# Chunk-selected attention feeding a top-1 expert layer: the first two head pairs in a new order, weights sent later, and expert tiles of two 64-row parts

## The chip, the core and the metric

The kernel runs on one core of a Trainium2 chip. The core has five engines that run side by side, each with its own queue of instructions: TensorE (PE, matmuls; its weight loads are listed as PEld), VectorE (DVE), ScalarE (ACT), GpSimd (POOL) and SyncE (SP, which only issues transfers). The metric is the device time of one execution in microseconds (us).

## The reference

For 4 batches, 8 heads, 768 positions and head size 64, attention is computed on chunks of 32 keys. Each query takes, of the chunks up to its own, the six with the highest upper bound, and attends to them alone. The rows of all heads (3072 tokens of 512) then go through one of eight experts each.

```python
k_min = np.min(k_chunks, axis=3)
k_max = np.max(k_chunks, axis=3)
ub = np.sum(np.maximum(q[:, :, :, None, :] * k_min[:, :, None, :, :], q[:, :, :, None, :] * k_max[:, :, None, :, :]), axis=-1)
ub = np.where(causal, ub, -1000000000.0)
top_chunks = np.argsort(ub, axis=-1)[..., -top_k:]
scores = scale * np.matmul(q, k.transpose(0, 1, 3, 2))
mask = sel & (pos[:, None] >= pos[None, :])
scores = np.where(mask, scores, -1000000000.0)
...
return np.matmul(attn, v).astype(np.float32)
...
expert_idx = np.argmax(logits, axis=1)
for e in range(E):
    mask = expert_idx == e
    xe = x[mask]
    h = np.maximum(xe @ w1[e], 0.0)
    ye = h @ w2[e]
    out[mask] = gate_w[mask, None] * ye
```

For the inputs of this case the eight experts get 85, 507, 932, 530, 163, 358, 285 and 212 tokens; after three of the four batches 45, 427, 850, 342, 99, 118, 274 and 149.

## The kernel before

**Stage one: 16 head pairs.** A pair is two heads of one batch. For each pair, `k_t` and `q_t` (L237, L266) transpose keys and queries on PE into the one bank `ps_t`; `k_red` (L243) takes each chunk's minimum and maximum on DVE; `k_out` (L261) copies the keys to KTE in four pieces on ACT; `q_v` and `q_va` (L279, L283) copy the queries to qT on DVE or ACT, `q_r` (L287) makes their positive part, `q_c` (L295) their bfloat16 copy on POOL. `kse` (L250) makes the two sides of the bound, `ub` (L382) multiplies them on PE, and `bound`, `maxes`, `choose` (L391 to L402) pick six chunks on DVE. The choice is transposed on PE and put (`put`, `put_to`) into rows 64 to 87 of QSB; the mask rows (`mask_rows`, L121) in the same rows of KTE make the score of a chunk that was not chosen strongly negative. `scores(i, u)` (L426) and `av(i, u)` (L457) do the attention in seven units of 384 queries by 128 keys; `v_t`, `v_c`, `vw`, `vw_c` add the gate's columns to V, and `norm` (L474) writes the rows of tokens.

Scores, sums over V and bounds use 64 columns of weights at a time (CW, L60), in two halves of PE's columns.

**Order.** PE and POOL run in the written order throughout, DVE and ACT too in the opening (L781 to L862). Pair 0 is prepared by `first` (L329) and `select_first` (L354), with idle matmuls (`idle`, L131) in PE's gaps; the keys of pair 1 are transposed after pair 0's choice, and the opening ends with the keys of pair 3 (`keys(3)`, L860). In the loop (L867) pair i is attended to, the bounds of pair i+1 computed, the queries of pair i+2 and the keys of pair i+3 transposed.

**Transfers.** `load` (L212) sends keys, queries and values by SP's queue, about two pairs ahead. `load_w` (L197) sends one of 32 pieces of the expert weights (512 KB as they land) by POOL's queue; `wq` (L751) says in which of a pair's four slots: three in the opening (EARLY), then spread over the pairs, none in the second pair of a later batch. `scatter` (L572) writes finished token rows, grouped by expert, to DRAM by the same queue, in slots of the next batch. POOL's third `q_c` of a pair waits for scatters that were issued in the pair before.

**Stage two: experts.** `table` (L596) counts on DVE how many tiles of 128 rows each expert has: full tiles of the first three batches first (11, NA), the rest (20, NB) after the last batch. Of these 31, 28 (JM) always run; the last three stand behind a branch. For a tile `gather` fetches the rows (POOL), `x_in` transposes them (SP), `up` (L706) and `down` (L724) are sixteen matmuls of 512 columns on all 128 columns of PE, with ACT's relu and a DMA transpose between; the weights' offset is read from `woff` at run time. The tiles overlap: `up(j)` is followed by `down(j - 2)` (L978 to L996).

## Time and profile before

| | us |
|---|---|
| median of 3 runs | 352.33 (351.08 to 354.74) |
| the profiled execution | 352.18 |
| its span, first to last instruction | 350.4 |
| PE busy | 316.2 |
| ACT busy | 205.0 |
| POOL busy | 182.5 |
| DVE busy | 175.0 |

The page also lists 224 matmuls of L731, eight for each of 28 tiles. A span's busy time is a mean over stages with different limits, so each stretch is read by itself. A chain of waits follows the last instruction back to what released it at each step: what stands in it set the time there. "Issue" in it is time in which an engine waited for nothing that the profile shows. The DMA share is the mean busy share of 16 DMA engines; overlapping packets can bring it over 1. Names such as ubp (bounds), kp, qp, vp (transposed keys, queries, values), ps (scores), po (sums over V), vwp (gate columns), ph and py (the halves of an expert tile) are those of the tiles written.

### The profile page before, as it was taken

How to read it: one execution, taken by the hardware profiler on the slowest of the kernel's cores; microseconds unless marked ns; L12 is line 12 of the kernel's file. 1: busy time of each engine (PE TensorE's matmuls, PEld its weight loads, DVE VectorE, ACT ScalarE, POOL GpSimd, SP SyncE). 2: the span in 40 equal slices, each digit the busy share in tenths (PEclk: the TensorE clock that was granted, in tenths of full speed). 3: DMA queues.
4: the chain of work that ended last, by engine and by line, in shares of the span. 5: the costliest groups of instructions: out<-in, count | busy, mean ns of one | idle time of the engine just before them, and what ended most of it. 6: DMA issues, size and time to landing. Idle time of an engine off the chain costs nothing.

```text
span 350.4 us, 12914 instructions
## 1 busy us (share of the span) xinstructions
PE 316.2 (90%) x5206; PEld 231.3 (66%) x5206; DVE 175.0 (50%) x671; ACT 205.0 (59%) x306; POOL 182.5 (52%) x332
## 2 busy tenths in 40 slices
PE   7776999989999969899979997977898999999992
PEld 3556788978988959789868896964343444444340
DVE  8557566756886647677666798555700000000000
ACT  2575777757767847767757765352444444455441
POOL 7631434634356736356655555836477455556232
PEclk9899899999999999999999999999999999999999
DMA  7995898978935999854899584326999999999982
GB/s 205 244 227 111 169 217 159 229 170 164 225 87 125 214 195 204 164 144 125 168 225 183 85 168 116 51 64 143 189 229 210 247 187 230 185 213 157 208 158 72
DMA packets 85979, 60.17 MB, mean 172 GB/s; under 512 B 73115, under 2 KB 73117, under 8 KB 85920
## 3 DMA queue, kind: packets, MB, share of 16 engines
q0 software_dynamic: 11392, 29.42, 41.4%
q1 hardware_dynamic: 74528, 29.91, 38.8%
q8 instruction: 43, 0.70, 0.8%
q14 instruction: 16, 0.13, 0.1%
HBM read 56.14 MB, written 10.51 MB: 190 GB/s over the span
## 4 chain that ended last, share of the span: by engine, by line
PE 68%; DVE 9%; issue 8%; DMA 6%; ACT 3%; POOL 3%; POOLq 1%; DVEq 0%; ACTq 0%; SPq 0%
PE po L469 23%; PE ph L714 9%; PE ps L440 9%; PE py L731 8%; PE ubp L387 5%; PE vp L306 4%; PE qp L271 3%; PE kp L241 3%; DMA xs_dram<-xrow,sli 3%; PE vwp L320 2%; ACT KTE L262 2%; POOL out_dram L738 2%; DMA hT<-h__4868 1%; DVE mm L246 1%; DMA spare<-xs_dram,grow 1%
## 5 line engine op out<-in xcount | busy, mean ns | idle before, releaser
L445 ACT ACTIVATE P<-ps 128x768 f32<-128x768 f32 x144 | 89.7, 666 | 57.5 <-PE ps L440 56.9
L469 PE MATMUL po<-V,P 128*64 128x73 f32 x2688 | 107.8, 229 | 7.6 <-issue 3.4
L469 PEld LDWEIGHTS po<-V,P 128*64 128x64 f32 x2688 | 97.8, 137 | 20.5 <-issue 10.3
L454 POOL TENSOR_SCALAR_AFFINE_SELECT P<-P 128x256 f32<-128x256 f32 x90 | 36.0, 415 | 81.6 <-ACT P L445 81.1
L731 PE MATMUL py<-w_all,hT 128*128 x224 | 52.7, 379 | 3.8 <-DMA hT<-h__5871 2.1
L440 PE MATMUL ps<-QSB,KTE 128*64 128x384 bf16 (+2 forms) x576 | 55.3, 292 | 0.7 <-ACT P L445 0.7
L731 PEld LDWEIGHTS <-hT 128*128 128x128 bf16 x224 | 21.9, 98 | 30.7 <-DMA hT<-h__5871 2.5
L262 ACT ACTIVATE KTE<-kp 64x384 bf16<-64x384 f32 x64 | 38.5, 602 | 4.2 <-PE kp L241 2.6
L297 POOL CAST QSB<-qT 64x384 bf16<-64x384 f32 x62 | 29.6, 502 | 15.2 <-DMA xs_dram<-xrow,sli 7.1
L714 PE MATMUL ph<-w_all,KTE 128*128 x120 | 28.3, 379 | 3.7 <-DVE lg L509 1.5
L246 DVE TENSOR_REDUCE mm<-kp 128x48 f32<-128x768 f32 x32 | 29.1, 946 | 0.9 <-PE kp L241 0.9
L440 PEld LDWEIGHTS <-KTE 128*64 128x64 bf16 x576 | 27.0, 110 | 1.8 <-issue 1.6
L575 POOL DMA_INDIRECT xs_dram<-xrow,sli x21 | 21.5, 1024 | 8.6 <-issue 5.2
L738 POOL DMA_INDIRECT out_dram<-V,ti x14 | 13.8, 988 | 22.0 <-ACT V L737 13.4
L714 PE MATMUL ph<-w_all,QSB 128*128 x104 | 24.6, 379 | 0.0
L314 DVE COPY vT<-vp 128x768 f32<-128x768 f32 x14 | 13.4, 957 | 22.2 <-PE vp L306 22.2
L387 PE MATMUL ubp<-ks,qT 128*64 128x48 f32 x320 | 20.4, 223 | 4.2 <-DVE ks L255 2.9
L714 PEld LDWEIGHTS <-KTE 128*128 128x128 bf16 x120 | 11.6, 97 | 18.3 <-issue 3.0
L387 PEld LDWEIGHTS ubp<-ks,qT 128*64 128x64 f32 x320 | 18.7, 139 | 5.0 <-POOL QSB L297 3.3
L387 PE MATMUL ubp<-kd,qA 128*64 128x48 f32 x320 | 20.5, 224 | 1.4 <-DVE kd L258 1.4
L205 POOL DMA_DIRECT2D w_all<-in_moe_w_dram x32 | 21.1, 661 | 0.2
L387 PEld LDWEIGHTS ubp<-kd,qA 128*64 128x64 f32 x320 | 18.7, 140 | 1.6 <-ACT P L445 1.1
(196 smaller groups left out, 426.2 us busy)
## 6 DMA issues: line engine op xcount, KB each, us to landing
w_all<-in_moe_w_dram POOLq DMA_DIRECT2D x32, 512.0 KB, 6.7
V<-in_v_dram SPq DMA_DIRECT2D x32, 192.0 KB, 5.3
k<-in_k_dram SPq DMA_DIRECT2D x8, 384.0 KB, 3.9
q<-in_q_dram SPq DMA_DIRECT2D x8, 384.0 KB, 4.7
w_all<-in_k_dram SPq DMA_DIRECT2D x8, 384.0 KB, 7.1
w_all<-in_q_dram SPq DMA_DIRECT2D x8, 384.0 KB, 4.3
xs_dram<-xrow,sli POOLq DMA_INDIRECT x21, 7.0
out_dram<-V,ti POOLq DMA_INDIRECT x14
```

What stands on the lines that cost most here:

```text
L205: d = nc.gpsimd.dma_start(out=dst, in_=src.rearrange("(c p) f -> p c f" if n < 2 else "(p c) f -> p c f", p=128))
L246: nc.vector.tensor_reduce(s["mm"][:, n].rearrange("p a c -> p (a c)"), s["kp"].rearrange("p j (c w) -> p c j w", w=CH // KG), AX.XY, (ALU. ...
L262: nc.scalar.activation(kte[0:64, hd, :].rearrange("p (r j z) -> p z r j", z=2, j=KG // 2)[:, z], s["kp"][64 * z:64 * z + 64, :, ts(hd, KR ...
L297: nc.gpsimd.tensor_copy(out=o_, in_=i_)
L387: nc.tensor.matmul(pu[64 * hd:64 * hd + 64, t].rearrange("p z n -> p (z n)"), lhsT=s[nm][:, ds(hd * 384 + t * 64, 64)], rhs=w_[:, hd], sta ...
L440: nc.tensor.matmul(pv[c:c + CW, hd, :], lhsT=kte[:, hd, ds(kb * 128 + c, CW)], rhs=qsb[:, hd, ds(qb * 384 + 384 - w, w)], start=True, stop ...
L445: nc.scalar.activation(P[:, :, ds(c0, w)], pv, AF.Exp)
L454: nc.gpsimd.affine_select(out=pd, in_=pd, pattern=[[0, 2], [1, 2], [2, 64]], compare_op=ALU.is_ge, fill=0.0, base=0, channel_multiplier=-1)
L469: nc.tensor.matmul(po[c:c + CW, t].rearrange("p a d -> p (a d)")[:, ds(hd * VW, VW)], lhsT=P[:, hd, ds(col + c, CW)], rhs=vt[:, kb, ds((1 ...
L575: d = nc.gpsimd.indirect_dma_start(out=xs_dram[:], out_offset=bass.IndirectOffsetOnAxis(ap=sli[:, u:u + 1], axis=0), in_=bst[b][f"xrow{u % ...
L714: nc.tensor.matmul(ph[:, fh, :], lhsT=xT[:, c, :], rhs=w_all[:, ds(wo + (c * F + fh * 512), 512)], start=(c == 0), stop=(c == NDC - 1), sk ...
L731: nc.tensor.matmul(py[:], lhsT=hT[:, c, :], rhs=w_all[:, ds(wo + (W1W + c * DM), DM)], start=(c == 0), stop=(c == NFC - 1))
```

## The change

- **Opening.** The keys of pair 1 are transposed into a score bank (`ps_s`, 2 banks) while pair 0's bounds are prepared, and leave it in pieces until the second score unit of pair 0. Pair 0's gate columns come ahead of its first score. All of pair 0's qT is made by ACT, all of its `q_c` by POOL. `first` and `select_first` are gone; `turn` and `put_half` are called from the order itself.
- **Fourth keys.** The keys of pair 3 are transposed and copied in pair 1 of the loop.
- **Constants.** cbias is made by one iota and one DVE instruction instead of one iota and ten. The mask rows of the second and third KTE are copied from the first by SP's queue; the zero fills of those buffers come after pair 0's `q_c`.
- **Weights.** No piece is sent in the opening's constants. `wq` now has two in pair 0, three in each of pairs 1 to 4, then one, two, two, three, one, three, two, and (with the last three) two, one, one.
- **Expert tiles.** After the 11 full tiles the rest is counted in parts of 64 rows (`part_table`). Seven tiles hold two parts of one expert. Eight mixed tiles hold one leftover part in rows 0 to 63, and in rows 64 to 127 one part of expert 0 to 7. 26 tiles always run, two stand behind the branch. In a mixed tile `up` and `down` issue each matmul twice, on 64 columns of weights each, the halves with different experts' w_all.

```diff
-    NB = NTOK // 128 + E - 1 - NA
+    NF = 9
+    NB = NF + E
     JT = NA + NB
-    JM = JT - 3
+    JM = JT - 2
     WE = 2 * DM * F // 128
     W1W = WE // 2
     WL = (E - 1) * WE
     CW = 64
     VW = D + 1 + E
-    EARLY = 3
...
-    def mask_rows(i):
+    def mask_rows():
         for hd in range(2):
-            nc.vector.tensor_scalar(KTE[i][64:64 + NCH, hd, :], colc[64:64 + NCH, :],
+            nc.vector.tensor_scalar(KTE[0][64:64 + NCH, hd, :], colc[64:64 + NCH, :],
                                     pm64[64:64 + NCH, 0:1], MASKV, ALU.is_equal, ALU.mult)
+
+    def more_mask_rows():
+        for i in (1, 2):
+            nc.sync.dma_start(out=KTE[i][64:64 + NCH], in_=KTE[0][64:64 + NCH])
...
+        iota(cbias[:], [[-4, NT - 1], [1, NCH]], base=-4)
...
-        for t in range(1, NT):
-            thr = const.tile([128, 1], FP32, name=f"thr{t}")
-            nc.vector.tensor_scalar(thr[:], chunk_p[:], float(4 * t), None, ALU.add)
-            nc.vector.tensor_scalar(cbias[:, t - 1, :], iota_c[:], thr[:, 0:1], NEG,
-                                    ALU.is_gt, ALU.mult)
-        mask_rows(0)
-        zero_half(KTE[1])
-        zero_half(KTE[2])
-        zero_half(QSB[1])
+        nc.vector.tensor_scalar(cbias[:], cbias[:], chunk_p[:, 0:1], NEG, ALU.is_gt, ALU.mult)
+        mask_rows()
...
-    def table(first):
...
+    def part_table():
...
+        nc.vector.tensor_scalar(ni[:], cnt[:], 63.0, None, ALU.add)
+        nc.vector.tensor_scalar(ni[:], ni[:], 6, None, ALU.logical_shift_right)
...
+        nc.vector.tensor_scalar(more[:], u0[:, 0:1], float(2 * (JM - NA - E)), None, ALU.subtract)
...
+    def col(j):
+        if j < NA + NF - 2:
+            return j
+        return j + 2 if j < JM else j - E
+
+    def parts(j, wo):
+        if NA + NF - 2 <= j < JM:
+            return ((wo, 0, 64), ((j - (NA + NF - 2)) * WE, 64, 128))
+        return ((wo, 0, 128),)
...
-                nc.tensor.matmul(ph[:, fh, :], lhsT=xT[:, c, :],
-                                 rhs=w_all[:, ds(wo + (c * F + fh * 512), 512)],
-                                 start=(c == 0), stop=(c == NDC - 1), skip_group_check=True)
+                for o_, lo, hi in parts(j, wo):
+                    nc.tensor.matmul(ph[lo:hi, fh, :], lhsT=xT[:, c, lo:hi],
+                                     rhs=w_all[:, ds(o_ + (c * F + fh * 512), 512)],
+                                     start=(c == 0), stop=(c == NDC - 1), skip_group_check=True)
...
-            nc.tensor.matmul(py[:], lhsT=hT[:, c, :], rhs=w_all[:, ds(wo + (W1W + c * DM), DM)],
-                             start=(c == 0), stop=(c == NFC - 1))
+            for o_, lo, hi in parts(j, wo):
+                nc.tensor.matmul(py[lo:hi, :], lhsT=hT[:, c, lo:hi], rhs=w_all[:, ds(o_ + (W1W + c * DM), DM)],
+                                 start=(c == 0), stop=(c == NFC - 1), skip_group_check=True)
...
-    slots = [4 * i + g for i in range(NP - 2) for g in range(4) if i < HP or i % HP != 1]
-    wq = EARLY * [-1] + [slots[n * len(slots) // (NW - 3 - EARLY)] for n in range(NW - 3 - EARLY)] + [4 * NP - 7, 4 * NP - 13, 4 * NP - 11]
+    pieces = {0: (2, 3), 5: (0,), 6: (0, 3), 7: (0, 3), 9: (0,), 11: (0, 3), 12: (0,)}
+    wq = [4 * i + g for i in range(NP - 3) for g in pieces.get(i, (0, 2, 3))] + [4 * NP - 7, 4 * NP - 13, 4 * NP - 11]
...
         load(0, "k")
         load(0, "q")
+        load(1, "k")
         load(0, "v")
         with tc.manual_schedule(engines={DVE, ACT}):
             idle = consts_first()
+            load(1, "q")
             p0, p, pj = prep[0], prep[1], prep[2]
+            p0["k_t"]()
+            load(2, "k")
+            p0["q_t"](ps_s.tile([128, 2, 512], FP32, tag="s", name="pq"))
             load(1, "v")
             load(2, "q")
             load(2, "v")
+            idle(3)
+            p0["k_red"](0)
+            p0["k_red"](1)
+            p0["q_va"]()
+            p0["q_r"]()
+            for n in range(4):
+                p0["q_c"](n // 2, n % 2)
+            zero_half(KTE[1])
+            zero_half(QSB[1])
+            zero_half(KTE[2])
+            more_mask_rows()
+            for n in range(4):
+                p0["k_out"](n // 2, n % 2)
+            p["k_t"](ps_s.tile([128, 2, 512], FP32, tag="s", name="pk"))
+            load(3, "k")
+            idle(6)
+            p0["kse"]()
+            p["k_red"](0)
+            p0["ub"]()
+            idle(2)
+            p0["bound"]()
+            p0["maxes"](1, 3)
+            p0["choose"](1, 3)
+            p0["v_t"]()
+            p["k_out"](0, 0)
+            p["k_out"](0, 1)
+            p0["v_c"](act=True)
+            p0["turn"](0)
+            p0["maxes"](3, 6)
+            p0["choose"](3, 6)
+            p0["put_half"](0)
+            idle(2)
+            p["k_out"](1, 0)
+            p0["vw"](ps_o, "o")
+            p0["vw_c"]()
+            scores(0, 0)
+            p["q_t"]()
+            load(3, "q")
+            p["k_red"](1)
+            p0["turn"](1)
+            p0["put_half"](1)
+            p["k_out"](1, 1)
+            scores(0, 1)
+            p["q_v"]()
+            p["q_r"]()
+            p["kse"]()
+            for n in range(4):
+                p["q_c"](n // 2, n % 2)
             consts_pool()
             consts_last()
+            weights(0)
+            av(0, 0)
             scores(0, 2)
+            pj["k_t"]()
+            load(4, "k")
+            pj["k_out"](0, 0)
+            pj["k_out"](0, 1)
+            av(0, 1)
+            pj["k_red"](0)
             scores(0, 3)
             norm(0, 0)
+            p["ub"]()
+            pj["k_out"](1, 0)
+            pj["k_out"](1, 1)
             scores(0, 4)
             p["bound"]()
             p["maxes"](1, 6)
             p["choose"](1, 6)
+            pj["k_red"](1)
+            weights(1)
             av(0, 2)
             scores(0, 5)
             av(0, 3)
+            weights(2)
             p["mask"]()
             p["put"]()
             scores(0, 6)
+            pj["kse"]()
+            p["v_t"]()
+            p["v_c"](act=True)
             av(0, 4)
             pj["q_t"]()
             load(4, "q")
+            pj["q_va"]()
             pj["q_r"]()
+            weights(3)
             av(0, 5)
...
+            if i == 1:
+                pj["k_t"]()
+                load(5, "k")
...
+            if i == 1:
+                pj["k_out"](0, 0)
+                pj["k_out"](0, 1)
```

**ACT in the opening.** KTE are the keys' copies of pairs 0, 1 and 2 (by number), pq the queries of pair 0, P the exponentials. Before, from the first copy on:

```order
L285 ACTIVATE qT<-pq 128x384
L289 ACTIVATE qA<-qT 128x768
L262 ACTIVATE KTE_105<-kp 64x384 x4
L301 ACTIVATE QSB_108<-qT 64x2x3x64 x2
L312 ACTIVATE vT<-vp 128x768
L445 ACTIVATE P<-ps 128x768
L445 ACTIVATE P<-ps 128x2x256
L445 ACTIVATE P<-ps 128x2x128
L262 ACTIVATE KTE_106<-kp 64x384 x4
```

Now, with pk for the keys of pair 1 in the score bank:

```order
L289 ACTIVATE qT<-pq 128x768
L293 ACTIVATE qA<-qT 128x768
L266 ACTIVATE KTE_107<-kp 64x384 x4
L266 ACTIVATE KTE_108<-pk 64x384 x2
L312 ACTIVATE vT<-vp 128x768
L266 ACTIVATE KTE_108<-pk 64x384
L408 ACTIVATE P<-ps 128x768
L266 ACTIVATE KTE_108<-pk 64x384
L408 ACTIVATE P<-ps 128x2x256
L408 ACTIVATE P<-ps 128x2x128
```

Three of pair 1's four copies moved ahead of the first exponential, the fourth ahead of the second.

**DVE at the first bounds.** mm are the key extremes, lo, ks and kd the sides of the bound, ubm the masked bounds. Before:

```order
L123 TENSOR_SCALAR KTE_105<-colc,pm_93 24x768 x2
L246 TENSOR_REDUCE mm<-kp 128x48 x2
L281 COPY qT<-pq 128x384
L253 COPY lo<-mm 64x96
L255 TENSOR_TENSOR ks<-mm,lo 64x2x24 x2
L256 TENSOR_TENSOR lo<-mm,lo 64x48
L258 TENSOR_TENSOR kd<-lo,ks 64x2x24 x2
L394 TENSOR_TENSOR ubm<-ubp,cbias 128x240
```

Now:

```order
L170 TENSOR_SCALAR cbias<-cbias,chunk_p 128x120
L125 TENSOR_SCALAR KTE_107<-colc,pm_92 24x768 x2
L250 TENSOR_REDUCE mm<-kp 128x48 x2
L257 COPY lo<-mm 64x96
L259 TENSOR_TENSOR ks<-mm,lo 64x2x24 x2
L260 TENSOR_TENSOR lo<-mm,lo 64x48
L262 TENSOR_TENSOR kd<-lo,ks 64x2x24 x2
L250 TENSOR_REDUCE mm<-pk 128x48
L357 TENSOR_TENSOR ubm<-ubp,cbias 128x240
```

The copy of qT left DVE, and one of the two reductions of pair 1's keys stands ahead of the masked bounds.

**PE in a tile behind the first 18.** These are the first matmuls of `up`, the ISA rows add up an address. Before:

```order
L707 TENSOR_LOAD woff
L714 ISA
L714 MATMUL ph<-w_all,KTE_107 128x512
L714 LDWEIGHTS KTE_107
L714 ISA
```

Now, in the first mixed tile:

```order
L762 TENSOR_LOAD woff
L770 ISA
L770 MATMUL ph<-w_all,KTE_109 64x512
L770 LDWEIGHTS KTE_109
L770 MATMUL ph<-w_all,KTE_109 64x512
L770 LDWEIGHTS KTE_109
L770 ISA
```

Each matmul became two, on 64 columns of weights; the second has a fixed address.

## Rows read from the trace of the kernel before

**Rows 1.** The page, busy us, share of the span and instructions of each engine.

```profile
PE 316.2 (90%) x5206; PEld 231.3 (66%) x5206; DVE 175.0 (50%) x671; ACT 205.0 (59%) x306; POOL 182.5 (52%) x332
```

**Rows 2.** Table by stretch: length, busy us of each engine, granted clock, DMA share, GB/s.

```profile
9.00:18.00 9.00, 7.04 (x68) 4.74 (x69) 5.28 (x23) 4.87 (x8) 5.61 (x22) 0.81 1.15 242
...
18.00:27.00 9.00, 6.47 (x115) 4.88 (x111) 4.66 (x12) 7.50 (x13) 3.37 (x8) 1.00 0.93 211
...
27.00:39.75 12.75, 10.64 (x201) 9.47 (x201) 8.52 (x31) 7.57 (x13) 2.87 (x6) 0.87 0.59 129
...
53.40:66.10 12.70, 12.70 (x299) 11.22 (x297) 8.62 (x31) 9.59 (x16) 6.72 (x15) 1.00 0.88 174
...
250.80:348.00 97.20, 90.92 (x417) 40.50 (x414) 5.34 (x33) 44.84 (x53) 52.36 (x52) 1.00 0.94 193
```

**Rows 3.** Chain of waits, opening: start us, us, what.

```profile
6.98 1.82 DVE mm L246 x2
...
8.80 0.46 DVE qT L281
...
11.23 1.66 PE ubp L387 x36
...
17.79 0.45 PE ps L440 x4
...
20.17 0.60 ACT KTE L262
```

**Rows 4.** Timeline: start us, us, engine, line, operation, in brackets idle before.

```profile
5.07 0.83 PE L241 MATMUL kp<-ident_f,k 96*128 96x96 f32 x8
...
12.93 0.41 DVE L394 TENSOR_TENSOR ubm<-ubp,cbias 128x240 f32<-128x240 f32 x1 [1.85 <-PE ubp L387]
...
15.49 0.58 DVE L350 COPY QSB<-pm 24x256 bf16<-24x256 bf16 x2 [0.46 <-PE pm L360]
...
39.75 0.82 PE L320 MATMUL vwp<-wgb,vT 128*64 128x16 f32 x24
...
53.40 0.83 PE L320 MATMUL vwp<-wgb,vT 128*64 128x16 f32 x24
```

**Rows 5.** Chain of waits, pairs 2 to 4.

```profile
61.18 0.91 PE po L469 x24
...
62.70 0.81 PE kp L241 x8
...
65.19 0.33 PE ps L440 x4
...
70.26 1.32 issue
...
83.80 1.15 PE ubp L387 x40
```

**Rows 6.** Chain of waits, experts: two halves of tiles.

```profile
250.84 1.73 PE ph L714 x8
...
252.57 1.73 PE py L731 x8
```

**Rows 7.** Timeline of DVE and POOL around the second table.

```profile
246.64 0.15 DVE L600 TENSOR_TENSOR cnt<-base_e,ebase 128x8 f32<-128x8 f32 x1
...
252.86 0.18 DVE L655 SCALAR_TENSOR_TENSOR grow<-inv,loc 128x20 int32<-128x20 f32 x1
...
267.49 1.04 POOL L681 DMA_INDIRECT KTE<-xs_dram,grow  x1 [0.30 <-issue]
```

**Rows 8.** DMA queues in pair 2 (53.40 to 66.10): packets, MB, share.

```profile
q0 software_dynamic: 478, 1.00, 50.1%
...
q1 hardware_dynamic: 1824, 1.18, 37.0%
```

**Rows 9.** Chain of waits and PE's timeline in pair 7.

```profile
118.07 8.87 DMA xs_dram<-xrow,sli
...
128.94 0.88 PE L306 MATMUL vp<-ident_f,V 128*128 128x128 f32 x6 [2.72 <-ACT qT L285]
```

More of the change, by code (lines that the diff above doesn't have):

```diff
@@ L101 @@
     base_e = const.tile([128, E], FP32)
-    jio = const.tile([128, NB], FP32)
+    jio = const.tile([128, NA], FP32)
+    pos = const.tile([128, NB], FP32)
+    p64 = const.tile([128, 1], FP32)
+    upper = const.tile([128, 4, E], FP32)
     tri8 = const.tile([128, E, E], FP32)
@@ L178, in consts_pool @@
         iota(ebase[:], [[NTOK, E]])
-        iota(jio[:], [[1, NB]])
+        iota(jio[:], [[1, NA]])
+        iota(upper[:, 0], [[1, E]])
+        for z in range(2):
+            iota(pos[64 * z:64 * z + 64, 0:NF], [[2, NF]], base=z)
+            iota(p64[64 * z:64 * z + 64, :], [[0, 1]], mul=1)
         for b in range(B):
@@ L799 @@
-            idle(2)
-            def filler():
-                idle(2)
-                p["k_t"]()
-                idle(2)
-            p0["select_first"](filler, idle, lambda: scores(0, 0), lambda: p["k_red"](0))
-            p["k_red"](1)
-            scores(0, 1)
-            load(3, "k")
-            for n in range(4):
-                p["k_out"](n // 2, n % 2)
-            p0["vw"]()
-            p0["vw_c"]()
-            scores(0, 2)
-            av(0, 0)
-            p["q_t"]()
-            load(3, "q")
@@ L974 @@
             tok(5)
-            for _ in table(False):
-                pass
+            part_table()
             def tiles(lo, hi):
@@ L997 @@
         dve.__exit__(None, None, None)
-    rest = nc.values_load(more[0:1, 0:1], min_val=NA - JM, max_val=JT - JM,
-                          skip_runtime_bounds_check_because="the table counts at most one part tile per expert")
+    rest = nc.values_load(more[0:1, 0:1], min_val=-2 * (NF - 2), max_val=4,
+                          skip_runtime_bounds_check_because="every expert leaves one part to a tile of its own")
     with tc.If(rest > 0):
```

292 lines of the change are left out of this document (149 added, 143 removed).

## The prediction

> **What bounds the kernel now.** I read the page's busy times first: TensorE (PE) works for 316.2 of 350.4 us, the next engine (ScalarE, ACT) for 205.0 [rows 1]. Then the table by stretch, which shows where it does not work: 7.0, 6.5 and 10.6 us of the stretches 9 to 18, 18 to 27 and 27 to 39.75 us, with a mean granted clock of 0.81, 1.00 and 0.87 there (part of the first and the last at 1.2 GHz, with gaps in PE's work before) [rows 2]. From 39.75 us, where the first pair of the steady loop adds its gate columns, PE is full: one pair takes 12.7 us where nothing disturbs it. From 250.8 us on the experts run at PE's pace, 90.9 busy us of 97.2 [rows 2]. So three things can move the time: the first 40 us (latency), the disturbed pairs, and the number of expert tiles. The chain of waits tells what orders the first stage [rows 3], the timeline gives its marks [rows 4], the chain of an undisturbed pair gives the price of PE's pieces [rows 5].
>
> **Opening, up to the first score.** Before, the score of pair 0 starts at 17.79 [rows 3]. Step by step in the new order:
> - The key extremes (L246) can start when the eight transposes end, 5.07 + 0.83 = 5.90 [rows 4], where they started at 6.98 [rows 3]: ten small VectorE (DVE) instructions for cbias become one, and the mask rows end earlier. Minus 1.08.
> - The copy of half of qT leaves DVE: minus 0.46 [rows 3]. ACT now makes all of qT and is done long before.
> - The bounds took 1.66 us for 36 pieces at the low clock [rows 3]; at the high one 40 take 1.15 [rows 5]. Second keys and six idle matmuls stand in PE's wait, so I take the high clock: minus 0.5.
> - So the bounds end near 10.9 in place of 12.9. From the start of the adds (12.93) to the end of the first put (15.49 + 0.58 = 16.07) lie 3.1 us [rows 4]; the same DVE work needs some 2.7, since PE's V transposes now hide under the maxima. First put done at 13.6, score at 13.7. Gone between put and score (16.07 to 17.79) are the second keys' transposes and four idle matmuls.
>
> That is 4.1 us. **From the first score to 39.75** lay 22.0 us. PE's work in the new order, at the high clock: four sets of transposes (queries and values of pair 1, keys and queries of pair 2) at 0.81, bounds 1.15, mask 0.3, eight score units at 0.33, seven sums over V at 0.91 [rows 5], together 13.7. Pair 0's gate columns and the fourth keys are no longer in it. Walking the order by hand leaves two waits of PE: the second score unit for ACT's fourth piece of second keys, whose bank it shares (0.4 us), and the third sum for the normalisation (0.8). With 1.5 us for what a walk by hand misses: 16.4, so the mark of 39.75 comes at 30.1. Minus 9.6 so far.
>
> **The fourth keys a pair later.** Pair 1 (13.65 us, 39.75 to 53.40 [rows 4]) gets eight transposes (0.81) and four ACT copies of 0.60 [rows 3, 5]. The copies delay its exponentials behind PE by at most 2.4; most hides, since ACT has slack in a 12.7 us pair. I take plus 0.9 (bounds 0.8 and 2.4). Opening in all: minus 8.7, bounds minus 4 (if the walk is 4 to 5 us short) and minus 11.
>
> **Mask rows by DMA, zero fills later, first weights later.** Two copies of 24 rows go by SyncE's queue between the loads of pair 2 and the keys of pair 3, which are wanted a pair later; the waiting copy holds only those. Nothing.
>
> **Tiles.** Before, 28 tiles ran. A tile's two halves take 1.73 us each, sixteen matmuls of 512 columns at 0.216 [rows 6]. Now JM is 26: 11 full, 7 pairs of parts, 8 mixed tiles whose 64-row halves belong to two experts. For the token counts of these inputs (85, 507, 932, 530, 163, 358, 285, 212) the seven pairs hold exactly the parts left over, so the two tiles behind the branch stay out. Two tiles fewer: 2 x 3.45 = minus 6.9. A mixed tile issues 32 matmuls of 64 columns of weights, in place of 16. Their price isn't in the trace; the nearest row is the score unit: four matmuls of 384 columns on 64-column halves take 0.33 us [rows 5], while one of 384 at 2.4 GHz takes 0.16. So two halves run at a time and their weight loads are hidden. There both halves stream the same columns; here they stream two experts' weights. The bounds do stream two heads' columns into the two halves, at 1.15/40 = 29 ns a piece [rows 5], but that is too near a load's price to prove it. I take the pair at the price of a full matmul. Twice the instructions on PE, beside a DMA share of 0.94 [rows 2], may cost a fetch stall or two: plus 1.0. Sum minus 5.9; bounds minus 6.9 and, halves one after the other, 8 x 3.45 - 6.9 = plus 20.7.
>
> The Trainium skill, "TensorEngine Tiling (Array Packing)", says under Restrictions that column tiling disables fast weight loads, and under Key Properties that changing the tiling mode drains the engine; by that rule the loads could come out from under the streams. The score row's 0.33 us shows them hidden.
>
> **Part table.** DVE's second table grows from 26 to 69 instructions. Before: 246.64 to 253.04, 0.25 us each [rows 7], so now to about 263.9. Behind it stand only row indices of later tiles; the first gather that reads it is issued at 267.49 [rows 7]. Hidden, by 3.6 us; without that cover each us late would cost up to one.
>
> **Weights from then on.** Three pieces are no longer sent in the opening; pairs 1 to 4 carry three each. In pair 2 of before, two pieces' worth (1.00 MB) took 50.1% and the loads 37.0% of 12.7 us [rows 8]: 3.2 us a piece, 4.7 the loads. Three pieces: 9.6 + 4.7 = 14.3 us of DMA in 12.7, a share of 1.13; the highest in the table is 1.15 [rows 2]. It just fits, and loads are sent a pair ahead. What suffers is what queues behind: a fetch like the stall of 1.32 [rows 5], or a scatter. In pair 7 GpSimd's casts waited for a scatter that took 8.87 us behind two pieces, and PE stood for 2.72 [rows 9]; the new list has one piece there, which is 3.2 us less: minus 2.7. Pair 10 now has the pattern that pair 6 had (slots 0, 2, 3): plus 0.5. Pairs 2 to 6: plus 2. Together about 0, bounds minus 3 and plus 6.
>
> The Trainium skill, "DMA: Bandwidth & Descriptors", section "Issuing engines are not separate DMA queues", says that transfers of all engines interleave on the same sixteen, which speaks against three pieces beside the loads. The trace agrees as far as the scatter's 8.87 us behind two pieces goes.
>
> **Sum.** The profiled run took 352.18 us, the median of the runs is 352.33; 352.2 - 8.7 - 5.9 + 0 = 337.6.
>
> **Rivals.**
> - Forecast: about 337.6, between 331 and 343. Chance 0.62.
> - The loads of the mixed tiles stand bare: 32 loads at 29 ns are 0.93 us a tile, 7.4 in all, and the saving is gone: 345. Against it the score unit. 0.10.
> - Three pieces a pair choke the queues: stalls of 1.3 to 2.7 in three or four of the pairs 2 to 6 and 11, plus 6: 344. For it the 1.13 above. 0.15.
> - The other side: halves with different streams don't overlap. Each mixed tile takes 6.9 us: 352.2 - 8.7 + 20.7 + 1 = 365. It decides from about 1.8 us more per mixed tile (14.6 saved, over 8). For it: no row with two streams that settles it. Against: the score unit's 0.33. 0.10.
> - The change doesn't shorten the experts: the last two tiles run after all, at least 6.9 us more, 345 or above. The counts speak against it. 0.03.
>
> **How the numbers follow.** About 1% is what a measurement of this kernel can tell from no change. The forecast and the two rivals near 345 are all faster than 348.7, but their upper ends reach it: faster 0.84, same 0.05, slower 0.11. The range is 330 (opening 11, tiles 6.9, queues 3, with a little left over) to 347; it leaves out the serial halves and the worst of the choked queues.
>
> **What would show it.** First score near 13.7; gate columns of pair 1 near 30 and of pair 2 near 44 to 45; no low clock between 9 and 39 us; each half of a mixed tile (tiles 18 to 25) at 1.73 us; the first gather of the part table not waiting for DVE; no wait of the casts in pair 7. Wrong would be: halves of mixed tiles near 3.5 us, or gate columns of pair 1 later than 35.

## The result

The changed kernel takes 340.94 us in the median of 4 runs (338.67 to 342.23), the kernel before 353.26 in the same comparison: a ratio of 0.9649, 95% interval 0.957 to 0.9728. Forecast were 337.6 and a range of 330 to 347. The profiled execution is the fastest of the four, 338.67 us with a span of 336.9; its spans are used below.

The page, TensorE's row (busy us, share, instructions) and the row of its granted clock in 40 slices:

```profile
PE 308.0 (91%) x5302; PEld 228.3 (68%) x5302; DVE 178.6 (53%) x694; ACT 200.7 (60%) x299; POOL 179.7 (53%) x335
...
PEclk9999999999999999999999999999999999999999
```

PE is busy 308.0 us in place of 316.2 [rows 1]. The table by stretch (busy us of PE, its loads, DVE, ACT and POOL, clock, DMA share, GB/s), against [rows 2]:

```profile
9.00:18.00 9.00, 8.26 (x130) 5.62 (x128) 7.42 (x26) 6.83 (x13) 4.13 (x9) 1.00 1.16 248
18.00:27.00 9.00, 8.18 (x176) 7.13 (x177) 8.24 (x27) 7.75 (x12) 7.15 (x32) 1.00 0.38 97
27.00:29.59 2.59, 2.59 (x59) 2.35 (x60) 0.97 (x5) 1.68 (x3) 0.55 (x1) 1.00 0.95 166
44.49:57.22 12.73, 12.73 (x299) 11.25 (x297) 8.64 (x31) 9.48 (x16) 6.61 (x15) 1.00 1.05 216
270.57:325.31 54.74, 54.26 (x354) 25.46 (x354) 2.08 (x13) 26.36 (x31) 27.60 (x28) 1.00 0.95 205
```

From 9 to 27 us PE now works 16.4 us of 18 where it worked 13.5, at a clock of 1.00 in place of 0.81 in the first half. An undisturbed pair is still 12.73 us (before 12.70), but the DMA share beside pair 2 is 1.05 in place of 0.88. The chain of waits in the opening, against [rows 3], and PE's marks behind it, against [rows 4]:

```profile
5.94 1.83 DVE mm L250 x2
...
10.23 1.27 PE ubp L350 x36
...
13.77 0.88 PE vwp L320 x24
14.65 0.34 PE ps L403 x4
```

```profile
29.59 0.83 PE L320 MATMUL vwp<-wgb,vT 128*64 128x16 f32 x24
...
36.64 0.88 PE L275 MATMUL qp<-ident_f,w_all 128*128 128x128 f32 x6 [1.30 <-ACT KTE L266]
...
44.49 0.83 PE L320 MATMUL vwp<-wgb,vT 128*64 128x16 f32 x24
```

The gate columns of pair 1 come at 29.59 in place of 39.75, those of pair 2 at 44.49 in place of 53.40. In between stands a new wait of 1.30 us, at the query transposes. The experts, against [rows 6] (`128*64` are the halves of mixed tiles; line 770 is the first half, 788 the second, one tile behind):

```profile
297.11 1.89 PE L788 MATMUL py<-w_all,hT 128*128 x8
298.93 1.92 PE L770 MATMUL ph<-w_all,KTE 128*64 x16
300.78 1.90 PE L788 MATMUL py<-w_all,hT 128*128 x8
302.61 1.92 PE L770 MATMUL ph<-w_all,KTE 128*64 x16
...
313.22 1.89 PE L770 MATMUL ph<-w_all,QSB 128*64 x16
314.95 1.89 PE L788 MATMUL py<-w_all,hT 128*64 x16
```

Where mixed halves follow each other, 1.73 us lie from one to the next (313.22 to 314.95), as for full ones. The part table and the first gather that reads it, against [rows 7]:

```profile
241.17 0.16 DVE L625 TENSOR_TENSOR tables<-base_e,ebase 128x8 f32<-128x8 f32 x1
...
254.19 0.18 DVE L700 SCALAR_TENSOR_TENSOR grow<-tables 128x17 int32<-128x17 f32 x1
...
261.81 1.03 POOL L726 DMA_INDIRECT KTE<-xs_dram,grow  x1 [0.30 <-issue]
```

And the chain in the pairs, against the stall of [rows 5] and the scatter of [rows 9]:

```profile
61.44 1.50 issue
...
143.17 2.21 issue
...
165.83 9.42 DMA xs_dram<-xrow,sli
...
187.39 1.45 issue
```

In pair 7 PE has no wait any more (GpSimd's casts still wait 1.43 us for a scatter there, 4.28 before). But pairs 3, 9, 11 and 12 have stalls of 1.3 to 2.2 us, and in pair 11 the scatter at 165.83 holds PE for another 1.70. In pairs 2 to 15 PE is busy 166.5 us in place of 165.5 and stands idle 12.0 in place of 9.5: of the 3.5 us that they lose, 2.5 are waits.

| stage | before | after | difference | forecast |
|---|---|---|---|---|
| to the gate columns of pair 2 | 53.40 | 44.49 | -8.9 | -8.7 |
| pairs 2 to 15 (gate columns of 2 to those of 15) | 175.05 | 178.51 | +3.5 | 0 (-3 to +6) |
| from there to the first expert matmul | 12.26 | 12.42 | +0.2 | - |
| experts, to the end of the span | 109.7 | 101.5 | -8.2 | -5.9 |
| span | 350.4 | 336.9 | -13.5 | -14.6 |

### The profile page after: what moved, and what is told of

Its sections match the earlier page's. It is cut to its first block, busy times and chain, and to the rows that moved or that the text cites. A ratio compares the mean times of both kernels' runs of the same rounds, so it can differ in the third digit from the quotient of the medians.

```text
span 336.9 us, 13066 instructions
## 1 busy us (share of the span) xinstructions
PE 308.0 (91%) x5302; PEld 228.3 (68%) x5302; DVE 178.6 (53%) x694; ACT 200.7 (60%) x299; POOL 179.7 (53%) x335
## 4 chain that ended last, share of the span: by engine, by line
PE 51%; DMA 16%; issue 14%; POOL 10%; DVE 5%; ACT 2%; POOLq 1%; DVEq 0%; SPq 0%; ACTq 0%
PE po L432 22%; PE ps L403 8%; DMA out_dram<-V,ti 6%; DMA xs_dram<-xrow,sli 5%; PE ubp L350 4%; PE qp L275 3%; PE vp L306 3%; PE kp L245 3%; PE vwp L320 3%; DMA KTE<-xs_dram,grow 2%; DMA more_x<-xs_dram,grow 2%; POOL out_dram L795 2%; POOL xs_dram L538 2%; DVE mm L250 1%; PE pw L139 1%
## 5 line engine op out<-in xcount | busy, mean ns | idle before, releaser
L417 POOL TENSOR_SCALAR_AFFINE_SELECT P<-P 128x256 f32<-128x256 f32 x90 | 36.8, 423 | 75.8 <-ACT P L408 75.4
L788 PE MATMUL py<-w_all,hT 128*128 (+2 forms) x272 | 49.3, 379 | 1.4 <-DMA hT<-h__4898 0.7
L788 PEld LDWEIGHTS <-hT 128*128 128x128 bf16 (+1 forms) x272 | 21.6, 103 | 25.8 <-DMA hT<-h__4898 1.1
L266 ACT ACTIVATE KTE<-kp 64x384 bf16<-64x384 f32 x60 | 36.2, 603 | 3.2 <-PE kp L245 1.9
L301 POOL CAST QSB<-qT 64x384 bf16<-64x384 f32 x64 | 30.4, 500 | 13.7 <-DMA xs_dram<-xrow,sli 8.6
L770 PE MATMUL ph<-w_all,KTE 128*128 (+2 forms) x152 | 26.5, 380 | 2.8 <-DVE lg L472 1.6
L250 DVE TENSOR_REDUCE mm<-kp 128x48 f32<-128x768 f32 x30 | 27.3, 949 | 2.1 <-PE kp L245 1.7
L314 DVE COPY vT<-vp 128x768 f32<-128x768 f32 x14 | 13.4, 958 | 22.4 <-PE vp L306 22.4
L795 POOL DMA_INDIRECT out_dram<-V,ti x13 | 12.8, 984 | 20.6 <-ACT V L794 13.6
L770 PE MATMUL ph<-w_all,QSB 128*128 (+1 forms) x120 | 22.7, 379 | 1.1 <-DMA QSB<-more_x 0.6
L770 PEld LDWEIGHTS <-KTE 128*64 128x64 bf16 (+1 forms) x152 | 11.2, 104 | 15.9 <-issue 3.2
```

What stands on the lines that cost most here:

```text
L250: nc.vector.tensor_reduce(s["mm"][:, n].rearrange("p a c -> p (a c)"), s["kp"].rearrange("p j (c w) -> p c j w", w=CH // KG), AX.XY, (ALU. ...
L266: nc.scalar.activation(kte[0:64, hd, :].rearrange("p (r j z) -> p z r j", z=2, j=KG // 2)[:, z], s["kp"][64 * z:64 * z + 64, :, ts(hd, KR ...
L301: nc.gpsimd.tensor_copy(out=o_, in_=i_)
L417: nc.gpsimd.affine_select(out=pd, in_=pd, pattern=[[0, 2], [1, 2], [2, 64]], compare_op=ALU.is_ge, fill=0.0, base=0, channel_multiplier=-1)
L770: nc.tensor.matmul(ph[lo:hi, fh, :], lhsT=xT[:, c, lo:hi], rhs=w_all[:, ds(o_ + (c * F + fh * 512), 512)], start=(c == 0), stop=(c == NDC ...
L788: nc.tensor.matmul(py[lo:hi, :], lhsT=hT[:, c, lo:hi], rhs=w_all[:, ds(o_ + (W1W + c * DM), DM)], start=(c == 0), stop=(c == NFC - 1), ski ...
```

## The experiments

The kernels of runs e1 to e4 shared one chip, on which the kernel before takes 353.2 us; e5 to e8 ran on one where it takes 363.6, e9 to e11 where it takes 363.9, e12 where it takes 364.3. Totals are therefore compared with the kernel before of the same group, and stages by their marks.

**e1: the tiles alone.** The kernel before with the new constants of the tiles, both tables, `col`, `parts` and the loops of `up` and `down`; no line of the opening or of the weight list.

> The kernel before with the new expert tiles and part table alone: opening and weight list are the old ones. Theory (the parts of the change add up): the pairs stay as before, the experts lose 8.2 us (from the first expert matmul to the end 109.7 before, 101.5 in the changed kernel), so about 344.1. Rival (the stage of the experts gains only because it starts in another state of the queues; the tiles alone are worth two tiles less the switching of the mixed ones, 6.9 - 0.5): about 346. Last rival: the later start of the 64-row tiles costs and nothing is left, 350 or more.

Measured: ratio 0.9812 (0.9742 to 0.9881), 346.21 us. Gate columns of pairs 1 and 2 at 39.74 and 53.28, pairs 2 to 15 174.87 us: all as before. The experts take 102.5 us, 7.2 less. That lies between the first two theories (8.2 and 6.4 less); the stage has waits of its own that differ from run to run.

**e2: the opening and the weight list alone.** The changed kernel with the old tiles.

> The changed kernel with the old tiles and the old part table: new opening, new weight list. Theory: gate columns of pair 1 near 29.6 and of pair 2 near 44.5 as in the changed kernel (8.7 to 8.9 us ahead of before), pairs 2 to 15 about 178.5 us against 175.05 before, experts as before: 352.2 - 8.9 + 3.5 = 346.8. Rival (the 3.5 us in the pairs come with the tile change, which lengthens the program that is fetched): pairs 2 to 15 back near 175, 343.5.

Measured: ratio 0.9873 (0.9806 to 0.9941), 348.67 us. Marks at 29.46 and 44.36, pairs 2 to 15 178.29 us. The pairs' loss stays without the new tiles: the rival falls. The two ratios multiply to 0.969, within the interval of the whole change: the parts add up.

**e3: the old list of weights.**

```
-    pieces = {0: (2, 3), 5: (0,), 6: (0, 3), ...}
-    wq = [4 * i + g for i in range(NP - 3) for g in pieces.get(i, (0, 2, 3))] + [...]
+    EARLY = 3
+    slots = [4 * i + g for i in range(NP - 2) for g in range(4) if i < HP or i % HP != 1]
+    wq = EARLY * [-1] + [slots[n * len(slots) // (NW - 3 - EARLY)] ...] + [...]
```

> The changed kernel with the old list of weights (three pieces at the end of the opening's constants, the others evenly over pairs 0 to 13, in place of three a pair from pair 1 on). Theory (three pieces a pair are what stalls the fetches): PE's stalls put to issue fall from about 8 us to 5 or less, pairs 2 to 15 take 175 in place of 178.5, the total falls by 2 to 3.5 us, less what the early pieces cost the opening (up to 1). Rival (the stalls come wherever a fetch meets a busy queue, and the amount of traffic is the same): pairs 2 to 15 stay at 177 or more, with stalls at other places, and the total within 1 us; the wait for a scatter returns to pair 7.

Measured: 339.89 us, ratio 0.9601 (0.9507 to 0.9694), not to be told from the changed kernel. Pairs 2 to 15 take 177.95; stalls are at other places (1.59, 0.56 and 1.28 in pairs 2 and 3), and GpSimd's wait for a scatter is back in pair 7 with 2.89. My theory, that three pieces a pair stall the fetches, falls: with two a pair the loss is nearly the same.

**e4: the halves of a mixed tile one after the other.**

The loops of `up` are turned in the same way as those of `down`, shown here:

```
-        for c in range(NFC):
-            for o_, lo, hi in parts(j, wo):
+        for o_, lo, hi in parts(j, wo):
+            for c in range(NFC):
```

> The changed kernel, but in a mixed tile all matmuls of the lower 64 columns are issued first and then all of the upper 64, where they alternate in the changed kernel. Same work, same count. Theory (two halves run at a time only where neighbours in the order are on different halves): each half of the 8 mixed tiles takes near 3.45 us in place of 1.73, plus 8 x 3.45 = 27.6: about 366. Rival (a 64-column matmul is cheap in itself, or the engine overlaps them however they are ordered): 1.73 a half, 339.

Measured: 351.13 us. Of the 12.5 us that its span is longer, 3.3 lie in the mixed tiles (307.21 to 341.31 from the first half of tile 18 to the last of tile 25, in place of 298.93 to 329.75). PE's timeline there:

```profile
307.21 2.81 PE L770 MATMUL ph<-w_all,KTE 128*64 x16
309.95 1.90 PE L788 MATMUL py<-w_all,hT 128*128 x8
...
318.14 0.40 PE L788 MATMUL py<-w_all,hT 128*64 x1
318.35 0.38 PE L770 MATMUL ph<-w_all,KTE 128*64 128x512 bf16 x1
318.38 0.38 PE L788 MATMUL py<-w_all,hT 128*64 x1
...
319.93 0.40 PE L770 MATMUL ph<-w_all,QSB 128*64 x1
```

Neither theory holds. A mixed half between full ones takes 2.74 us (307.21 to 309.95), not 3.45 and not 1.73: the upper half starts before the lower one's last matmuls end. Where mixed halves follow each other, the last matmuls of the upper half of `ph` run beside the first of the lower half of the next `py` (three of each; the first rows are those at 318.35 and 318.38), and a half takes 1.79 (318.14 to 319.93). So two column halves with different streams do run at a time, also when their matmuls are some places apart in the order; the alternating order of the changed kernel is worth 1 us per half only where a full tile is next.

This run also shows what a stall can bring after it. The table by stretch around its longest (the clock is the third number from the end):

```profile
62.00:63.00 1.00, 0.48 (x17) 0.36 (x13) 0.66 (x2) 0.00 (x0) 1.00 (x3) 1.00 1.06 221
63.00:64.00 1.00, 0.00 (x0) 0.00 (x0) 0.00 (x0) 0.00 (x0) 0.53 (x1) 1.00 1.04 223
64.00:65.00 1.00, 0.00 (x0) 0.00 (x0) 0.00 (x0) 0.00 (x0) 0.00 (x0) 0.85 1.26 226
65.00:66.00 1.00, 0.93 (x15) 0.94 (x17) 0.00 (x0) 0.00 (x0) 0.00 (x0) 0.50 0.86 168
71.00:72.00 1.00, 1.00 (x13) 0.81 (x13) 0.16 (x1) 0.31 (x1) 0.52 (x2) 0.74 0.00 0
```

PE stood for 2.58 us; the clock fell to 0.50 (1.2 GHz) at 64.7 and came back at 71.5. Pair 3 took 18.46 us, in place of 14.43 in the changed kernel.

**e5: every second piece of weights left out.**

```
-            if wq[n] == slot:
-                load_w(n)
+            if wq[n] == slot and n % 2 == 0:
+                load_w(n // 2)
```

> The changed kernel with every second piece of weights left out: 16 pieces in place of 32, at every second place of the list; experts 4 to 7 compute with the weights of expert 3. Theory (PE's stalls put to issue and the wait for a scatter are instruction fetches and rows that queue behind a DMA near its limit): with 8.4 MB less in pairs 0 to 13 the stalls in pairs 2 to 15 fall from 8.1 us to under 2.5 and no wait of a scatter is left; pairs 2 to 15 near 168 to 170 in place of 178.5, the whole near 328 to 330. Rival (the fetches stall for a reason of their own, by the order of the code): stalls stay at 6 us or more, pairs 2 to 15 at 176 or more.

Measured: pairs 2 to 15 take 171.43 us, their issue stalls come to 2.4 us. PE's two longest waits in them:

```profile
131.64 0.87 PE L306 MATMUL vp<-ident_f,V 128*128 128x128 f32 x6 [2.24 <-ACT qT L289]
...
150.37 1.17 PE L432 MATMUL po<-V,P 128*64 128x73 f32 x29 [1.19 <-issue]
```

The stalls shrink with the bytes, so the rival falls; against my theory a wait of 2.24 us is left (the chain leads from it to a scatter that took 8.49 us), and the pairs take 171.4 us and not 168 to 170.

**e6: mixed tiles as full ones.**

```
     def parts(j, wo):
-        if NA + NF - 2 <= j < JM:
-            return ((wo, 0, 64), ((j - (NA + NF - 2)) * WE, 64, 128))
         return ((wo, 0, 128),)
```

> The changed kernel with tiles 18 to 25 computed as full tiles of 16 matmuls on 128 columns, with the expert of the lower half for all 128 rows, so that the upper half's rows are computed with another expert's weights. What the mixed form costs is the difference in time from the first half of tile 18 to the last half of tile 25 (298.93 to 329.75, 30.8 us, in the changed kernel). Theory (a mixed half costs what a full one does, 1.73, and each change between the two forms 0.1): 16 x 1.727 + waits, 0.5 to 0.6 us less. Rival (twice the instructions stall the fetch): 1 us or more less. In either case the whole moves by less than 1.5 us.

Measured, on PE's timeline (tile 18's first half is at 305.77; tile 24's, at 327.30, waits for the transfer of its rows and comes 2.53 us behind the half ahead of it, 0.80 more than the usual 1.73):

```profile
305.77 1.89 PE L768 MATMUL ph<-w_all,KTE 128*128 x8
...
327.30 1.89 PE L768 MATMUL ph<-w_all,KTE 128*128 x8 [0.64 <-DMA KTE<-spare]
```

From the first half of tile 18 to that of tile 24 lie 12 halves: 20.73 us without those 0.80, 21.20 in the changed kernel (298.93 to 320.13). The mixed form costs 0.47 us there, about 0.1 at each of four changes of form, seen in the rows at 298.93 to 302.61 as 1.85 and 1.83 in place of 1.73. The fifth change, ahead of 298.93, adds 0.09 (297.11 to 298.93 is 1.82): 0.56 in all, as the theory expected.

**e7: a sum ahead of pair 1's query transposes.**

```
             scores(i, 4)
+            if i == 1:
+                av(i, 2)
             if pj:
                 pj["q_t"]()
...
-            av(i, 2)
+            if i > 1:
+                av(i, 2)
```

> The changed kernel with one move in pair 1: its third sum over V is issued ahead of the query transposes of pair 3, in place of behind them. In the changed kernel PE stands 1.30 us there for ScalarE's copies of the fourth keys, which hold the bank. Theory (that wait is what pair 1 pays, and the sum is ready by then): pair 1 falls from 14.9 to 13.8 to 14.0 us and the rest stays, 0.9 us off the whole, too little for the ratio to tell but for the marks. Rival (the sum waits for its own exponentials, which the copies delay as well): pair 1 stays at 14.6 or more.

Measured: pair 1 takes 14.72 in place of 14.90, the rival's side, though not by its reason:

```profile
34.94 0.93 PE L432 MATMUL po<-V,P 128*64 128x73 f32 x24
36.42 0.87 PE L275 MATMUL qp<-ident_f,w_all 128*128 128x128 f32 x6 [0.55 <-ACT KTE L266]
...
38.27 0.87 PE L306 MATMUL vp<-ident_f,V 128*128 128x128 f32 x6 [0.54 <-ACT qT L289]
```

The sum runs (34.94). But the transposes still wait 0.55 for the copies, and the next user of the same bank, the value transposes, now waits 0.54 for ScalarE's copy of the queries: the wait moved down the chain of the bank. Ratio 0.9714 (0.962 to 0.9808), against 0.9766 (0.970 to 0.9831) of the unchanged one beside it: not told apart.

**e8: the changed kernel again.** Of the four runs of the changed kernel above, the profiled one has a mean granted clock of 0.999, the other three of 0.984 to 0.990.

> The changed kernel again, for its ratio beside the kernel of one move, and for the granted clock. [...] Rival (the lower clock is set by the opening): the opening's marks move as well, first score later than 15, gate columns of pair 1 later than 31.

Measured: 353.35 us, ratio 0.9766, on a chip that is slower by 10 to 12 us with either kernel. Marks at 29.40, 44.30 and 223.92: up to pair 15 this chip loses 0.9 us. The loss begins there: the first expert matmul comes at 243.21, 19.3 us behind that last mark where the first chip needed 12.4 (and the experts then take 106.2 us in place of 101.5). PE's timeline in pair 15:

```profile
234.08 0.39 PE L432 MATMUL po<-V,P 128*64 128x73 f32 x5 [0.36 <-issue]
234.80 0.35 PE L432 MATMUL po<-V,P 128*64 128x73 f32 x4 [0.32 <-issue]
235.53 0.36 PE L432 MATMUL po<-V,P 128*64 128x73 f32 x4 [0.38 <-issue]
```

After every four or five matmuls it stands for 0.32 to 0.38 us with nothing to wait for, one such pause every 0.73 us or so, and from 236.4 on the clock is at 0.50. Why, no run here tells. The marks of the opening do not move, so the rival falls; that the clock makes the spread of the four runs on the first chip fits (338.67 at a mean clock of 0.999; 340.25, 341.63 and 342.23 at 0.990, 0.984 and 0.989), but not in order, and the low stretches of those three runs were not profiled.

**e9: no idle matmuls in the opening.** The lines `idle(3)`, `idle(6)` and twice `idle(2)` behind the first nine are taken out.

> The changed kernel without the thirteen idle matmuls that stand between its opening's steps (the nine at the very start stay). Theory (the opening's gain is partly that PE's clock no longer falls, and the idle matmuls see to it): the granted clock shows 0.5 somewhere between 9 and 40 us, and the gate columns of pair 2 come at 45.5 to 48 in place of 44.5. Rival (the new order keeps PE busy enough without them): the clock stays at 1.00, the marks move by less than 0.6, if at all to the earlier.

```profile
9.00:18.00 9.00, 7.07 (x124) 5.49 (x125) 7.54 (x28) 6.70 (x12) 4.05 (x9) 1.00 1.17 249
18.00:27.00 9.00, 8.38 (x178) 7.23 (x176) 8.25 (x26) 7.56 (x12) 7.06 (x31) 1.00 0.39 101
27.00:40.00 13.00, 11.70 (x259) 10.10 (x259) 6.91 (x28) 10.29 (x15) 4.32 (x11) 1.00 1.06 229
```

Measured: the clock is 1.00 throughout (the third number from the end), and the marks are 29.40 and 44.30. The rival holds: the new order keeps the clock, not these thirteen idle matmuls (the nine at the very start were still there).

**e10: the fourth keys back in the opening.**

```
             av(0, 5)
+            keys(3)
...
-            if i == 1:
-                pj["k_t"]()
-                load(5, "k")
```

> The changed kernel with the fourth keys back at the end of the opening (transposes and copies before the loop, as in the kernel before) in place of inside pair 1. Theory (0.81 us of transposes cost the same in either place, and pair 1 also pays 1.3 us for the bank, which the opening's end pays as well): the gate columns of pair 1 come 0.8 to 2.5 later than 29.6, pair 1 is back near 12.7 to 13.0, and the gate columns of pair 2 stay at 44.5 within 0.7. Rival (the move to a later pair is a gain of its own): gate columns of pair 2 at 45.5 or later.

Measured, from the gate columns of pair 0 (14.46, 0.7 late, as in e3 and e4) to those of pair 2: 31.03 us, 30.72 in the changed kernel. The opening's part grows by 1.1, pair 1 falls by 0.8 to 14.13, since a wait stands there still, now for the exponentials behind the copies:

```profile
31.36 0.82 PE L320 MATMUL vwp<-wgb,vT 128*64 128x16 f32 x24
...
33.67 0.52 PE L403 MATMUL ps<-QSB,KTE 128*64 128x384 bf16 x4 [1.14 <-ACT P L408]
```

So moving the fourth keys is worth 0.3 us. Taken as it was written, the mark of pair 2 (45.49 for 44.5) lies 1.0 late, outside the theory's 0.7 and at the rival's edge; without the 0.7 that this run loses before its first mark the theory holds, except that pair 1 does not come back to 12.7.

**e11: four pieces moved to pairs 12 and 13.**

```
-    pieces = {0: (2, 3), 5: (0,), ..., 11: (0, 3), 12: (0,)}
+    pieces = {0: (2, 3), 2: (0, 2), 3: (0, 2), 5: (0,), ..., 10: (2, 3), 11: (3,), 12: (0, 1, 2), 13: (0, 2)}
```

> The changed kernel with four pieces of weights sent later: one each from pairs 2, 3, 10 and 11 to pairs 12 (two) and 13 (two), where the DMA queues stand idle most of the time. Theory (the pairs lose in proportion to the bytes that meet them early): stalls put to issue and scatter waits in pairs 2 to 12 fall by 2 to 4 us, pairs 2 to 15 take 175 to 176.5 in place of 178.5, the whole gains 2 us, ratio to before near 0.96. Rival (a fetch meets a busy queue wherever the pieces lie): pairs 2 to 15 within 1 us of 178.5.

Measured: pairs 2 to 15 take 178.22 us, and a stall of 2.69 stands in pair 9:

```profile
146.56 0.26 PE L350 MATMUL ubp<-kd,qA 128*64 128x48 f32 x2 [2.69 <-issue]
```

The rival holds. The ratio is 0.9619 (0.9549 to 0.9689), as the theory forecast for the whole, though not by way of the pairs. Its interval overlaps that of the changed kernel on the first chip (0.957 to 0.9728) but not that of e8 (0.970 to 0.9831), which ran on another chip of the slow kind. Of the 3.7 us between the spans of these two profiled executions the pairs make only 1.4, and 2.7 lie behind them, where both kernels are the same: that this list is better is not shown.

**e12: 28 pieces.**

```
     assert len(wq) == NW
+    for slot in (4 * 2 + 3, 4 * 4 + 3, 4 * 8 + 3, 4 * 10 + 3):
+        wq.remove(slot)
+    NW = len(wq)
```

> The changed kernel with four pieces of weights (2.1 MB) left out, one each of pairs 2, 4, 8 and 10; expert 7 computes with the weights of expert 6. Pairs 2 to 15 then move 28.0 MB, as in the kernel before, where the changed kernel moves 30.1. Theory (the 3.5 us that these pairs lost are the price of the 2.1 MB which the shorter opening no longer carries): pairs 2 to 15 take 175 to 176.5 us, against 178.5 to 179.8 with all pieces, and the stalls put to issue come to 4 to 5 us in place of 6.3 to 8.1. Rival (they were lost by the place of the pairs in time against the fetches, not by the bytes): 178 or more.

Measured: 176.86 us, between the two: 1.7 below the changed kernel on its first chip, 2.8 below e8. Stalls of 5.7 us and a scatter wait of 2.07. This run and e8 each have 3.4 us at a clock of 0.50 in these pairs, the changed kernel on its first chip and the kernel before have none; by an estimate from that length it costs up to half of it, 1.7 us, so without it e12 would lie between 175.2 and 176.9. What the DMA moved in pairs 2 to 15, in the kernel before, in the changed one (with its queue of instructions), and here:

```profile
DMA packets 27206, 28.02 MB, mean 160 GB/s; under 512 B 19792, under 2 KB 19792, under 8 KB 27169
```

```profile
DMA packets 28055, 30.14 MB, mean 169 GB/s; under 512 B 19861, under 2 KB 19861, under 8 KB 28016
...
q8 instruction: 30, 0.49, 1.1%
```

```profile
DMA packets 27234, 28.06 MB, mean 159 GB/s; under 512 B 19796, under 2 KB 19796, under 8 KB 27196
```

All profiled executions in one table (stalls are PE's idle times put to issue; scatter waits those of the value transposes, which lead back by ScalarE to GpSimd's casts; both those of 0.2 us or more; e8's 7.1 has in it a stall of 0.81 at 132.74 that the 6.3 of e12's expectation left out). The low clock is the time at 0.50 within these pairs.

| kernel | MB in pairs 2 to 15 | stalls | scatter waits | low clock | pairs 2 to 15 |
|---|---|---|---|---|---|
| e5 | 22.4 | 2.4 | 2.2 | 0 | 171.4 |
| before | 28.0 | 4.7 | 2.7 | 0 | 175.1 |
| e1 | 28.1 | 3.1 | 2.7 | 3.4 | 174.9 |
| e12 | 28.1 | 5.7 | 2.1 | 3.4 | 176.9 |
| e3 | 29.6 | 5.9 | 2.9 | 0 | 178.0 |
| e6 | 30.1 | 6.3 | 2.2 | 3.4 | 178.1 |
| e2 | 30.1 | 7.4 | 1.8 | 0 | 178.3 |
| after | 30.1 | 8.1 | 1.7 | 0 | 178.5 |
| e8 | 30.1 | 7.1 | 2.5 | 3.4 | 179.6 |
| e7 | 30.1 | 6.1 | 3.1 | 6.8 | 179.8 |
| e10 | 30.1 | 8.5 | 2.2 | 3.4 | 180.5 |
| e9 | 30.1 | 5.8 | 3.9 | 10.2 | 182.9 |
| e4 | 30.1 | 8.3 | 2.8 | 10.2 | 184.3 |
| e11 | 30.2 | 7.2 | 1.5 | 0 | 178.2 |

All kernels with the new opening and every piece of weights lie at 178.0 or more, with 5.8 to 8.5 us of stalls. At 30.1 MB the time still differs by 6 us from run to run, and the longest times go with the longest stretches of low clock.

What the stalls are can be read packet by packet. The queue of instructions (q8) moves packets of 16,384 bytes, 30 of them in these pairs, one every 6 us or so. In the changed kernel:

| packet of q8, start to end | stall of PE, start to end | from the packet's end to the stall's end |
|---|---|---|
| 60.56 to 61.53 | 61.44 to 62.94 | 1.4 |
| 96.00 to 96.97 | 97.76 to 98.31 | 1.3 |
| 129.51 to 130.54 | 131.05 to 132.09 | 1.5 |
| 143.13 to 144.09 | 143.17 to 145.39 | 1.3 |
| 172.49 to 173.43 | 173.50 to 174.82 | 1.4 |
| 186.61 to 187.54 | 187.39 to 188.84 | 1.3 |

Over all fourteen profiled executions, each of the 64 stalls of 0.5 us or more in pairs 2 to 15 ends 1.2 to 1.7 us behind the end of such a packet. Waits put to another cause end anywhere from 0.0 to 5.6 us behind one. So these stalls are waits for instructions. The pauses of e8 in pair 15 are another thing: they end 0.1 to 2.3 us behind a packet.

## Why the forecast was right, step by step

**First score.** Forecast 13.7, measured 14.65. The key extremes start at 5.94 (forecast 5.90) and the bounds run at the high clock. But they end at 11.50, not 10.9: the small DVE steps ahead of them (lines 257 to 262) take 2.3 us where the same steps took 1.9, for a reason that no run here shows, and the bounds themselves 1.27 for an expected 1.15. From the first add to the end of the first put lie 2.7 us, as forecast (11.53 to 14.23). The last 0.4 are pair 0's gate columns (13.77 to 14.65), which now stand ahead of the score: the walk took them out of the part behind the score and forgot them in the part ahead of it.

**To pair 1's gate columns.** Forecast 16.4 us, measured 15.1 (14.65 to 29.76 on the chain, 14.46 to 29.59 on the timeline). Of the two waits found by hand one is there, that of the third sum for the normalisation, 0.60 for 0.8:

```profile
22.50 0.99 PE L432 MATMUL po<-V,P 128*64 128x73 f32 x24 [0.60 <-DVE lgt L461]
```

The second score unit doesn't wait for ScalarE; two small waits that the walk did not have (0.16 and 0.21) stand elsewhere, and the allowance of 1.5 us was nearly all too much. That the mark came out right, 30.1 for a measured 29.76, is in part luck: 0.95 late and 1.3 early cancel.

**Fourth keys.** Forecast +0.9, measured +1.25 (14.90 for 13.65). The size was near, the mechanism another: not late exponentials but the bank, which passes from the keys to the queries to the values. E7 shows that chain, e10 that the move itself is worth 0.3 us.

**Clock.** No low clock between 9 and 39 us, as forecast; e9 shows that the order holds it without the idle matmuls between its steps, e1 that the old opening keeps its 0.81 and 0.87 with the new tiles.

**Mask rows, zero fills.** Nothing of them shows in the opening's chain.

**Tiles.** Forecast -5.9, measured -8.2 (e1: -7.2). Two tiles are 6.9; the mixed form costs 0.56 (e6) where 1.0 was allowed for fetch stalls, and no such stall came in the mixed tiles. Most of the rest are waits of PE in the stage, 5.9 us before and 3.6 after by the timelines, which no part of the change was meant to move: that much of the gain is luck. The three together would make -8.6; the 0.4 left over is not explained. The step that carried the risk, both halves at the price of one, holds at 1.73. By the Trainium skill, "TensorEngine Tiling (Array Packing)", section Key Properties, a change of the tiling mode drains the engine: the trace agrees in that each change costs about 0.1 us. The section Restrictions of the same page of the Trainium skill says that column tiling disables fast weight loads; here that costs nothing that the 1.73 would show.

**Part table.** 69 instructions in 13.2 us (241.17 to 254.37), 0.19 each and not 0.25 (the trace before shows 29 in its 6.4 us, not 26: 0.22 each); the first gather that reads it (261.81) comes 7.4 us later.

**Weights.** This is the step that was mis-sized: about 0 forecast, +3.5 measured, inside its bounds. Pair 7's scatter went as told (15.50 to 12.70, -2.8 for -2.7). Pairs 2 to 6 cost 1.2 us for an estimated 2, pair 10 nothing for 0.5. Not in the sum were pairs 9, 11 and 12: +2.4, +1.0 and +1.7, pairs with one or two pieces, where I looked for none. The working judged each pair by its own list; e3 and e11, with other lists, lose the same. What the kernels of the new opening with all pieces share is that the stage moves 29.6 to 30.2 MB where it moved 28.0: an opening shorter by 9 us carries less (e3, with the old list, moves 29.6), and the new list sends five pieces ahead of pair 2 where the old one sent eight. E5 shows that far fewer bytes mean fewer stalls. E12, with the bytes of before, wins back 1.7 to 2.8 of the 3.5 us, so the rest may hang on where in time the fetches meet the transfers, or on the low clock of that run; this is open.

By the Trainium skill, "Runtime: NRT & Kernel Launch", section "Instruction fetch mechanics", an engine's sequencer fetches its instructions by a DMA queue of its own while it executes, and the cost is mostly hidden. The trace agrees as to the queue (q8, 0.49 MB in these pairs); hidden the fetch is not, at 2.4 to 8.5 us of stalls. That PE waits for these packets is shown by their times; that the bytes of the other queues make them late is argued from the table, since no run shows when a fetch was asked for. The places recur (pair 3 has a stall in every execution), but which other fetches stall, and for how long, differs between runs of the same kernel.

The rival of the choked queues (stalls of 1.3 to 2.7 us in three or four pairs, plus 6) came half true: stalls of that size stand in four pairs, though two of them in pairs that it did not name, and the pairs lost 3.5.

**Sum and range.** The profiled run, 338.67, lies 1.1 above the sum; the errors are -0.2, -2.3, +3.5 and +0.2. That the sum is so near is luck: the fewer waits of the experts and the stalls of the pairs, neither of them in the sum at its size, cancel. The median lies 2.3 higher still, and the forecast had no term for runs with stretches of low clock behind a stall.

## What to carry to other kernels

When a stage that waits is shortened, its transfers do not get shorter: count the bytes of the next stage again, with all that the shortened one no longer carries, before taking the whole gain. Judge DMA queues near their limit by the bytes of the stage, not by the list of one pair, and look for packets of the instruction queue just before a stall that nothing else explains. Two half-width matmuls with different operands cost here what one full matmul costs if they alternate between the column halves (1.73 us a half tile); issued half after half they cost nearly the same beside their like (1.79), but not beside a full tile (2.74).
